# Longer q and k reads, reordered on the way out of PSUM, in a kernel of windowed attention and an ELU MLP

## The chip, the cores and the metric

One core of one Trainium2 chip runs the kernel. The metric is the device time of one execution in microseconds (us). Runs of one kernel agree within 2%. The calls ran on different chips, each with runs of the kernel before beside it; these stay within 401.3 to 409.0 us. The profile times are one profiled execution, about 2 us shorter than the run's own time.

Engine names in the profile: PE is TensorE (matmul), PEld its weight loads, DVE is VectorE, ACT is ScalarE, POOL is GpSimd, SP is SyncE, which issues DMAs. "PEclk" is the clock that TensorE was granted, 1.0 being full.

## The reference, cut to what matters

```python
batch, n_heads, seq, head_dim = 8, 8, 576, 64        # q, k, v: (8, 8, 576, 64) fp32
# down-sampled attention: q, k, v averaged over 4 tokens, 144 x 144 softmax, repeated 4 times
# local attention:        576 x 576 softmax, masked to |i - j| < 4
x = (out_up + out_local), to (8 * 576, 512)          # 4608 tokens
h = x @ w_in                                         # (512, 2048)
g = where(h > 0, h, exp(min(h, 0)) - 1)              # ELU
return g @ w_out                                     # (2048, 512)
```

Attention of a batch has to be done before the MLP can take the tokens of that batch. The kernel cuts the 4608 tokens into nine MLP tiles of 512. It works through the eight batches in pairs of heads (four pairs a batch).

## The kernel before

Q, k and v come in with one token of 64 fp32 values (256 B) as the contiguous run. Blocks of 96 tokens are transposed on TensorE by a matmul with the identity; the averages over four tokens are further columns of that same matmul. ScalarE and VectorE copy the results out of PSUM in the order in which they lie.

```python
ap=[[D, n], *blocks, [1, D]]                         # load: 256-byte runs, 96 tokens on 96 partitions
...
for c in range(NB):                                  # transposes; QI = identity | averages of 4
    nc.tensor.matmul(tq[:, c // 3, QW * (c % 3) : QW * (c % 3) + QW], q16[:, c, :, :], QI[:], ...)
...
nc.scalar.copy(out=qt[:], in_=tq[:, :, 0 : 3 * QW])
```

An MLP tile consists of 16 hidden blocks (`mm1`) and 16 output blocks (`mm2`), each of four matmuls of 512 columns. The hidden accumulator is one PSUM bank, and two of them are used in turn. Each is taken from the pool:

```python
def mm1(t, fc):
    ...
    tag = "misc" if t < 2 and fc % 2 else "hp"
    hp = ps.tile([128, TBLK], FP32, tag=tag, bufs=2, name="hp")
    for dc in range(DMC):
        nc.tensor.matmul(hp[:], WI[:, dc, 128 * fc : 128 * fc + 128], x[:, dc, :], ...)
    e = sb.tile([128, TBLK], FP16, tag="e", bufs=3, name="e")
    nc.scalar.activation(out=e[:], in_=hp[:], func=AF.Exp)
    nc.vector.tensor_scalar(out=e[:], in0=e[:], scalar1=1.0, scalar2=-1.0, op0=AB.min, op1=AB.add)
    nc.vector.scalar_tensor_tensor(out=gts[t][:, fc, :], in0=hp[:], scalar=0.0,
                                   op0=AB.max, in1=e[:], op1=AB.add)
```

Waits between engines are not written by hand: the tile framework records which instructions read and write each tile and puts in the semaphores. The program order on each engine is set by a list of events with times. Batches 1 to 7 are woven into the MLP of earlier tiles.

The softmax here doesn't subtract the row's maximum and nothing guards it: scores larger than these inputs give would overflow.

## Time and profile before

| | us |
|---|---|
| median of 2 runs | 404.04 (402.66 to 405.41) |
| profiled span | 401.8 |
| first hidden block with all its inputs | 48.6 |
| from when on TensorE is dense | about 141 |
| four matmuls of 512 columns, dense | 0.86 |

The stage view of the kernel before gives, for each stretch of the span, the busy time and number of instructions of each engine, then the granted clock, the DMA engines' busy share, and GB/s.

```profile
0.00:49.00 49.00, 22.97 (x252) 16.12 (x253) 13.87 (x25) 15.36 (x29) 24.74 (x35) 1.00 0.95 204
49.00:141.00 92.00, 75.81 (x741) 41.35 (x740) 61.88 (x109) 49.84 (x96) 43.96 (x56) 0.91 0.90 180
141.00:340.00 199.00, 196.45 (x1798) 102.14 (x1796) 153.06 (x275) 116.67 (x217) 70.03 (x96) 1.00 0.57 122
```

The first pair of numbers after the length is PE. TensorE is 99% busy from 141 to 340 us, so with the work of TensorE as it is, time can be won only before 141 us. DMA is nearly saturated up to 141 us, although it moves only 180 to 204 GB/s; most of its packets are under 512 B, as the next view shows.

The packet line of the page before and the rows of its group view that the change touches (engine, operation, output and inputs, count, then busy time and mean ns of one, then idle time before and what ended it):

```profile
DMA packets 138082, 53.81 MB, mean 134 GB/s; under 512 B 122580, under 2 KB 131388, under 8 KB 138044
L368 PE MATMUL hp<-xt,WI 128*128 128x512 f16 x576 | 150.9, 389 | 4.5 <-DVE gt L377 2.5 <-POOL xt L352 2.0
L182 ACT CAST qt<-tq 128x720 f16<-128x720 f32 x32 | 24.3, 760 | 30.7 <-PE tq L176 27.3 <-issue 2.3
L192 ACT CAST kt<-tk 128x612 f16<-128x612 f32 x32 | 21.8, 680 | 0.1
L263 DVE RECIPROCAL rc<-den 128x288 f16<-128x288 f32 x8 | 15.6, 1949 | 1.7 <-PE den L257 1.7
```

A copy out of PSUM costs about 0.7 us. The time line of TensorE shows the first hidden block getting its last input at 48.63 us and, late in the run with no attention left, hidden (`hp`) and output (`op`) blocks following each other every 0.86 us:

```profile
48.63 4.00 PE L368 MATMUL hp<-xt,WI 128*128 128x512 f16 x9 [0.69 <-POOL xt L352]
345.81 1.03 PE L368 MATMUL hp<-xt,WI 128*128 128x512 f16 x4
346.67 1.03 PE L388 MATMUL op<-WO,gt 128*128 128x512 f16 x4
347.54 1.03 PE L368 MATMUL hp<-xt,WI 128*128 128x512 f16 x4
```

### The profile page before, as it was taken

To read this page: it belongs to the slowest core of one execution; us is meant where nothing else is said; L and a number is where in the kernel's file an instruction comes from. 1 tells how busy PE (TensorE), PEld (TensorE's weight loads), DVE (VectorE), ACT (ScalarE), POOL (GpSimd) and SP (SyncE) were. 2 spreads that over 40 slices of the span, in tenths; PEclk is the share of its full clock that TensorE was granted. 3 is DMA by queue.
4 is the path that set the end of the run, shared out by engine and by line. 5 is a ranking of instruction groups with operands and counts; after the bars stand their busy time and mean duration, and the time that the engine had idled before them with its cause. 6 is when DMAs were issued, how large, how long until landed. Compare 5 with 4: busy or idle time off the path is not lost.

```text
span 401.8 us, 8092 instructions
## 1 busy us (share of the span) xinstructions
PE 353.0 (88%) x3052; PEld 185.6 (46%) x3052; DVE 254.4 (63%) x460; ACT 203.8 (51%) x377; POOL 138.7 (35%) x184
## 2 busy tenths in 40 slices
PE   1465688687986899999999999999899899999996
PEld 1352345343553455555545554555454444444442
DVE  0134599732586797697778769886886585555510
ACT  1462157535385376747564855667375334444321
POOL 3365755460850581075028304820450050000000
PEclk9999999968999799999999999999999999999999
DMA  6998999965966980796199639926820310100112
GB/s 121 189 253 258 190 215 234 265 126 134 198 139 130 189 176 16 172 231 125 28 195 217 118 78 194 226 64 121 172 79 33 102 53 28 49 29 28 52 54 78
DMA packets 138082, 53.81 MB, mean 134 GB/s; under 512 B 122580, under 2 KB 131388, under 8 KB 138044
## 3 DMA queue, kind: packets, MB, share of 16 engines
q1 hardware_dynamic: 129420, 47.62, 55.0%
q10 hardware_dynamic: 8624, 5.68, 6.6%
q8 instruction: 24, 0.39, 0.4%
q14 instruction: 14, 0.11, 0.1%
HBM read 43.33 MB, written 9.95 MB: 133 GB/s over the span
## 4 chain that ended last, share of the span: by engine, by line
PE 67%; DMA 12%; POOL 6%; issue 4%; DVE 4%; SPq 3%; ACTq 2%; ACT 1%; POOLq 0%; DVEq 0%
PE op L388 29%; PE hp L368 25%; PE sc L204 2%; PE tk L186 2%; PE tq L176 2%; DVE e L374 2%; PE tq L171 2%; PE lg L325 2%; POOL xt L352 2%; DMA w_170<-in_moe_w_in_dram 2%; DMA rcb<-rd 2%; SPq L149 2%; ACTq L276 2%; DMA w_161<-in_moe_w_in_dram 1%; DMA w_207<-in_moe_w_out_dram 1%
## 5 line engine op out<-in xcount | busy, mean ns | idle before, releaser
L368 PE MATMUL hp<-xt,WI 128*128 128x512 f16 x576 | 150.9, 389 | 4.5 <-DVE gt L377 2.5
L388 PE MATMUL op<-WO,gt 128*128 128x512 f16 x576 | 147.7, 385 | 4.7 <-POOL WO L119 3.8
L373 ACT ACTIVATE e<-hp 128x512 f16<-128x512 f32 x144 | 85.7, 601 | 109.5 <-PE hp L368 90.8
L377 DVE SCALAR_TENSOR_TENSOR gt<-hp,e 128x512 f16<-128x512 f32 x144 | 99.6, 692 | 5.4
L374 DVE TENSOR_SCALAR e<-e 128x512 f16<-128x512 f16 x144 | 63.8, 443 | 51.5 <-ACT e L373 50.5
L368 PEld LDWEIGHTS <-WI 128*128 128x128 f16 x576 | 54.5, 99 | 71.7 <-issue 13.4
L388 PEld LDWEIGHTS <-gt 128*128 128x128 f16 x576 | 54.6, 99 | 68.8 <-issue 7.6
L232 DVE TENSOR_TENSOR mex<-pex,MASK 102x1152 f16<-102x1152 f16 x32 | 29.6, 926 | 40.3 <-ACT pex L222 40.2
L352 POOL TENSOR_TENSOR xt<-ln,gn 128x512 f16<-128x512 f16 (+7 forms) x64 | 42.0, 688 | 34.7 <-DVE ln L343 34.7
L222 ACT ACTIVATE pex<-sc 102x576 f16<-102x576 f32 x64 | 41.4, 647 | 22.3 <-PE sc L214 22.3
L182 ACT CAST qt<-tq 128x720 f16<-128x720 f32 x32 | 24.3, 760 | 30.7 <-PE tq L176 27.3
L394 ACT COPY os<-op 128x512 f32<-128x512 f32 x36 | 21.2, 588 | 25.3 <-PE op L388 25.3
L204 PE MATMUL sc<-qt,kt 64*102 64x96 f16 x384 | 19.1, 226 | 11.5 <-DVE vd L184 6.0
L184 DVE CAST vd<-tq 72x256 f16<-72x256 f32 x32 | 13.2, 413 | 22.3 <-ACT qt L182 22.3
L204 PEld LDWEIGHTS <-kt 64*102 64x102 f16 x384 | 14.4, 135 | 25.8 <-ACT kt L192 12.6
L226 ACT ACTIVATE dex<-sc 72x288 f16<-72x288 f32 x64 | 25.8, 404 | 0.0
L343 DVE TENSOR_TENSOR ln<-lg,rcb 128x576 f16<-128x576 f32 x32 | 23.9, 748 | 0.0
L192 ACT CAST kt<-tk 128x612 f16<-128x612 f32 x32 | 21.8, 680 | 0.1
L176 PEld LDWEIGHTS <-VR 102*72 102x72 f16 x192 | 14.2, 123 | 5.7 <-issue 3.9
L263 DVE RECIPROCAL rc<-den 128x288 f16<-128x288 f32 x8 | 15.6, 1949 | 1.7 <-PE den L257 1.7
L340 DVE TENSOR_TENSOR gn<-lg,rcb 128x144 f16<-128x144 f32 x32 | 9.6, 301 | 5.7 <-POOL xt L352 3.0
L194 DVE CAST kd<-tk 128x144 f16<-128x144 f32 x32 | 9.6, 300 | 1.7 <-ACT kt L192 0.5
(361 smaller groups left out, 265.7 us busy)
## 6 DMA issues: line engine op xcount, KB each, us to landing
out_dram<-os SPq DMA_DIRECT2D x36, 256.0 KB
rcb<-rd ACTq DMA_DIRECT2D x14, 288.0 KB
rcb<-rd ACTq DMA_DIRECT2D x14, 72.0 KB
w_149<-in_moe_w_in_dram SPq DMA_DIRECT2D x1, 512.0 KB
w_152<-in_moe_w_in_dram SPq DMA_DIRECT2D x1, 512.0 KB
w_155<-in_moe_w_in_dram SPq DMA_DIRECT2D x1, 512.0 KB
w_158<-in_moe_w_in_dram SPq DMA_DIRECT2D x1, 512.0 KB
w_161<-in_moe_w_in_dram SPq DMA_DIRECT2D x1, 512.0 KB
```

What stands on the lines that cost most here:

```text
L182: nc.scalar.copy(out=qt[:], in_=tq[:, :, 0 : 3 * QW])
L204: nc.tensor.matmul(sc[e][0:KW, c // 3, QB * (c % 3) : QB * (c % 3) + QB], kt[r, c // 3, c % 3, :], qt[r, c // 3, QW * (c % 3) : QW * (c % ...
L222: nc.scalar.activation(out=pex[:, e, :].rearrange("p (g u) -> p g u", g=2), in_=sc[e][0:KW, :, 0:HB], func=AF.Exp, scale=SCALE,)
L226: nc.scalar.activation(out=dex[:, e], in_=sc[e][0:KG, :, HB : HB + SD], func=AF.Exp, scale=SCALE,)
L232: nc.vector.tensor_tensor(out=mex[:], in0=pex[:], in1=mk2, op=AB.mult)
L343: nc.vector.tensor_tensor(out=ln[:].rearrange("p (g u) -> p g u", g=2), in0=lg[:, :, 0:HB], in1=rcb[:, j, 0:S].rearrange("p (g u) -> p g u ...
L352: nc.gpsimd.tensor_tensor(out=xt(t)[:, j, t0 - TBLK * t : t1 - TBLK * t], in0=ln[:, a:z], in1=_rep4(gn[:, a // 4 : z // 4]), op=AB.add,)
L368: nc.tensor.matmul(hp[:], WI[:, dc, 128 * fc : 128 * fc + 128], x[:, dc, :], start=(dc == 0), stop=(dc == DMC - 1),)
L373: nc.scalar.activation(out=e[:], in_=hp[:], func=AF.Exp)
L374: nc.vector.tensor_scalar(out=e[:], in0=e[:], scalar1=1.0, scalar2=-1.0, op0=AB.min, op1=AB.add)
L377: nc.vector.scalar_tensor_tensor(out=gts[t][:, fc, :], in0=hp[:], scalar=0.0, op0=AB.max, in1=e[:], op1=AB.add)
L388: nc.tensor.matmul(op_[:], gts[t][:, fc, 128 * tt : 128 * tt + 128], WO[:, fc, :], start=(fc == 0), stop=(fc == FCN - 1),)
```

## The change

The intent is to shorten the front. Q and k are loaded with six consecutive tokens per partition (1.5 KB runs). The transposes then give token order "r, t" (token 6t + r), and the copy out of PSUM puts it right ("untangle"). Averages over four are no longer columns of the transposes but sums of the reordered tiles (on VectorE for batches 0 and 1, on GpSimd after that). Denominators are packed into 72 columns by 96 small matmuls, so that the reciprocal has 72 columns instead of 288. Batches 0 and 1 run by themselves, apart from the MLP, with hidden tile 0 between them. For that, PSUM is laid out by hand as four tiles of two banks, and the accumulators become halves of those.

```diff
-    def two(name):
-        return ps.tile([128, 2, 512], FP32, tag="two", bufs=2, name=name)
+    PA = ps.tile([128, 1024], FP32, tag="PA", bufs=1, name="PA")
+    PB = ps.tile([128, 1024], FP32, tag="PB", bufs=1, name="PB")
+    PM = ps.tile([128, 1024], FP32, tag="PM", bufs=1, name="PM")
+    PH = ps.tile([128, 1024], FP32, tag="PH", bufs=1, name="PH")
... (loads)
+                    ap=[[NR * D, NP], [S * D, 2], [1, NR * D]],
... (reordering copy)
+        copy(
+            out=qk[:, i, PAD : PAD + S].rearrange("p (t r) -> p r t", r=NR),
+            in_=tp[:, 0 : 128 * NR].rearrange("p (r t) -> p r t", r=NR)[:, :, 0:NP],
+        )
... (hidden blocks)
-        tag = "misc" if t < 2 and fc % 2 else "hp"
-        hp = ps.tile([128, TBLK], FP32, tag=tag, bufs=2, name="hp")
+        if t == 0:
+            hp = ((PH, PM)[fc % 2])[:, 512 * (fc // 2 % 2) : 512 * (fc // 2 % 2) + 512]
+        else:
+            hp = PH[:, 512 * (fc % 2) : 512 * (fc % 2) + 512]
... (order)
+    early(0, between0)
+    ...
+    for s in range(FCN):
+        mm1(0, s)
+    ...
+    early(1, lambda: None)
```

## The prediction

> **What bounds the kernel now.** The stage table (busy time in windows) shows two regimes. From 141 us to the end TensorE is 94 to 100% busy at full clock; the chain of waits there is almost only the two MLP matmul lines (four 512-column matmuls take 0.86 us, 215 ns each). A period of 16 hidden blocks, 16 output blocks and one batch of attention takes 37.7 us, 27.6 of it MLP, so about 10.1 us is one batch's attention. Nothing in the change shortens that. Nine tiles (248 us) and eight batches (81 us) need 329 us of the 402 us span; the other 73 us lie before 141 us: some 35 us before the first MLP block has all its inputs (48.6 us), because q, k, v arrive in 256-byte packets and TensorE did about 10 us of work, and some 25 us in 48 to 141 us (waits for casts, for DMA and for vd/kt copies, and granted clock 0.66 in 80 to 90 us, 0.83 in 120 to 140 us).
>
> **Front.** Before, a pair of heads arrived every 5 to 8 us (DMA share about 1.0 at 189 GB/s in 10 to 20 us, small halo transfers issued for 1.3 to 1.8 us each). 1.5 KB runs should go at about 300 GB/s (258 GB/s at share 0.85 for the 1 KB weight runs, 30 to 40 us); the Trainium skill, "DMA: Bandwidth & Descriptors", Specifications, asks for at least 512 B. Then q, k are in by about 12 us, v by 20. The loop over pairs is bound by VectorE: copy 0.76, sums of 4 about 1.3 (1152 elements at one per cycle: tensor_reduce has only the 1x mode by "VectorE: DVE Perf Modes", tier table; an estimate), mask 0.76, so about 3 us a pair. Sums, denominators (cold clock), spreading and outputs end near 37 us: the MLP starts about 10 us earlier.
>
> **Given back.** Hidden tile 0 runs alone, bound by VectorE (0.29 to 0.75 + 0.69 us a block): about 18 us for 13.8 of matmuls. Batch 1 is then done with no MLP beside it: four pairs at 3 us, denominators, spreading, outputs, about 26 us for 10 us of TensorE work; MLP tile 1 starts near 82 us. In front of batch 2 stand eight weight casts of 1.04 us on GpSimd, and its slots are one apart, so TensorE waits some 10 us more. Denominators become 96 small matmuls (16 of 144 columns took 0.36 us, 23 ns each): about +1 us a batch; narrower transposes save 0.5. The reciprocal falls from 1.95 to about 0.6 us, on an engine that does not bound. GpSimd sums (about 1.2 + 0.7 us) lengthen transposes-to-scores; that chain had about 0.8 us slack: 0 to 6 us in all.
>
> **Sum.** 82 + 298 dense + 4 tail + about 10 stall is 394 in the trace; retuned constants speak for less, stalls for more. Predicted median 393 us.
>
> **Right if** the profile shows the first hidden block fully fed at 34 to 41 us; packets under 512 B cut by more than half; TensorE under half busy for about 25 us between tile 0 and tile 1; then a stretch above 95%, at 37.5 to 39 us a period; reciprocal near 0.6 us.
>
> **Wrong if** batch 1 alone takes under 18 us or batch 2 does not stall (then 375 to 380), or if every scores block waits for the GpSimd sums (1 us each adds 20 us and it is slower than before), or if strided copies out of PSUM cost far more than 0.7 us.
>
> Chances: faster by over 2% 0.56, within 2% 0.33, slower 0.11. Range 375 to 409 us.

## The result, and the profile after

The changed kernel takes 603.9 us (601.09 and 606.71), against 404.04 us before. It is 1.496 times as slow, with a 95% interval of 1.475 to 1.517. Here and below, a ratio is the mean time of one kernel's fast runs over that of the other's fast runs in the same rounds, so it is not quite the ratio of the medians quoted.

The stage view of the kernel after, same columns:

```profile
0.00:40.00 40.00, 22.12 (x339) 16.53 (x340) 22.78 (x25) 21.26 (x31) 17.59 (x32) 1.00 0.90 253
88.00:160.00 72.00, 49.12 (x573) 27.39 (x572) 27.87 (x44) 42.37 (x53) 40.07 (x47) 0.67 0.46 121
160.00:460.00 300.00, 208.01 (x1933) 100.20 (x1932) 133.06 (x231) 156.12 (x203) 100.22 (x131) 0.90 0.28 75
460.00:599.00 139.00, 98.47 (x564) 41.55 (x562) 47.61 (x95) 35.59 (x61) 5.28 (x8) 0.99 0.10 34
```

The front did get shorter: the first hidden block has all its inputs at about 40 us, not 48.6. But the dense regime is gone. TensorE is 69% busy from 160 to 460 us and 71% from 460 us on, where hardly any attention is left. The page and the group view name two things:

```profile
DMA packets 73236, 53.34 MB, mean 89 GB/s; under 512 B 46842, under 2 KB 66410, under 8 KB 73194
L447 PE MATMUL PH<-xt,WI 128*128 128x512 f16 x544 | 160.8, 421 | 128.0 <-DVE gt L456 121.9 <-POOL xt L420 4.8
L214 ACT CAST qk<-PA 128x576 f16<-128x576 f32 x32 | 71.8, 2244 | 1.3 <-PE PA L208 1.3
L214 ACT CAST qk<-PB 128x576 f16<-128x576 f32 x24 | 50.2, 2090 | 13.5 <-PE PB L237 13.2
L230 POOL TENSOR_TENSOR s<-qk 128x576 f32<-128x576 f16 x24 | 27.5, 1144 | 172.2 <-ACT qk L214 172.2
```

First, the hidden blocks of TensorE waited 121.9 us for VectorE's `gt`, the last reader of the hidden accumulator; before it was 2.5 us. Second, the reordering copy takes 2.1 to 2.2 us instead of 0.7, and on ScalarE 24 + 32 of them are 122 us of work. The late time line of the kernel after, where no attention runs, shows the first of these alone (the top line is the first fully fed hidden block):

```profile
40.21 0.58 PE L447 MATMUL PH<-xt,WI 128*128 128x512 f16 x1 [0.69 <-POOL xt L420]
521.01 1.02 PE L447 MATMUL PH<-xt,WI 128*128 128x512 f16 x4 [0.88 <-DVE gt L456]
521.87 1.03 PE L467 MATMUL PM<-WO,gt 128*128 128x512 f16 x4
522.07 0.60 ACT L452 ACTIVATE e<-PH 128x512 f16<-128x512 f32 x1 [2.17 <-PE PH L447]
522.70 0.29 DVE L453 TENSOR_SCALAR e<-e 128x512 f16<-128x512 f16 x1 [1.74 <-ACT e L452]
523.02 0.69 DVE L456 SCALAR_TENSOR_TENSOR gt<-PH,e 128x512 f16<-128x512 f32 x1
523.77 1.02 PE L447 MATMUL PH<-xt,WI 128*128 128x512 f16 x4 [0.88 <-DVE gt L456]
```

Read it as a loop. A hidden block at 521.01, its exponential at 522.07, VectorE until 523.71, and only then the next hidden block at 523.77. The period is 2.76 us for a hidden and an output block, where it was 1.73. The accumulators alternate between two banks, so the next block need not wait for the reader of this one. The compiled program says that it was made to. I listed, for some hidden blocks, which VectorE instruction their semaphore wait stands for (this comes from building the kernels, not from the profile; offsets are in words of the tile, 512 being the second bank):

```
after:   matmul I-2425 writes PH at 512, waits for I-2393, which reads PH at   0
         matmul I-2463 writes PH at   0, waits for I-2432, which reads PH at 512
before:  matmul I-3723 writes hp_3722,   waits for I-3678, which reads hp_3670 (two blocks back)
         matmul I-3786 writes hp_3785,   waits for I-3691, which reads hp_3683 (two blocks back)
```

In the changed program a block waits for the reader of the other half, the block just before it. 128 hidden blocks of the changed program had a wait for such a reader, each for the other half of its own tile; in the kernel before 95 had one, each for an earlier tile. Two halves of one tile are no double buffer here.

### The profile page after: what moved, and what is told of

Read it like the earlier page. It is cut to its first block, busy times and chain, and to the rows that moved or that the text cites. A ratio compares the mean times of both kernels' runs of the same rounds, so it can differ in the third digit from the quotient of the medians.

```text
span 599.3 us, 8991 instructions
## 1 busy us (share of the span) xinstructions
PE 408.6 (68%) x3600; PEld 202.0 (34%) x3600; DVE 266.6 (44%) x440; ACT 279.8 (47%) x383; POOL 177.1 (30%) x234
## 4 chain that ended last, share of the span: by engine, by line
PE 33%; DVE 20%; ACT 20%; issue 8%; POOL 4%; DMA 1%; ACTq 0%; DVEq 0%; POOLq 0%
PE PH L447 17%; ACT qk L214 10%; PE PM L467 10%; DVE gt L456 9%; DVE e L453 7%; ACT e L452 7%; DVE ln L411 2%; PE PB L265 1%; POOL WO L145 1%; POOL xt L420 1%; ACT os L473 1%; DVE gn L408 1%; PE PB L237 1%; DMA v<-in_v_dram 1%; PE PB L277 1%
## 5 line engine op out<-in xcount | busy, mean ns | idle before, releaser
L447 PE MATMUL PH<-xt,WI 128*128 128x512 f16 x544 | 160.8, 421 | 128.0 <-DVE gt L456 121.9
L452 ACT ACTIVATE e<-PH 128x512 f16<-128x512 f32 x136 | 86.0, 633 | 224.7 <-PE PH L447 224.7
L467 PE MATMUL PM<-WO,gt 128*128 128x512 f16 x576 | 160.8, 409 | 7.8 <-DVE rc L337 4.4
L447 PEld LDWEIGHTS <-WI 128*128 128x128 f16 x576 | 58.3, 104 | 225.4 <-issue 175.9
L456 DVE SCALAR_TENSOR_TENSOR gt<-PH,e 128x512 f16<-128x512 f32 x136 | 94.1, 692 | 5.1
L230 POOL TENSOR_TENSOR s<-qk 128x576 f32<-128x576 f16 x24 | 27.5, 1144 | 172.2 <-ACT qk L214 172.2
L214 ACT CAST qk<-PA 128x576 f16<-128x576 f32 x32 | 71.8, 2244 | 1.3 <-PE PA L208 1.3
L214 ACT CAST qk<-PB 128x576 f16<-128x576 f32 x24 | 50.2, 2090 | 13.5 <-PE PB L237 13.2
L190 POOL CAST q<-q 96x768 f16<-96x768 f32 x32 | 27.1, 847 | 23.8 <-issue 19.7
L190 POOL CAST k<-k 96x768 f16<-96x768 f32 x32 | 27.5, 860 | 2.3 <-DMA k<-in_k_dram 2.2
L197 POOL CAST v<-v 112x768 f16<-112x768 f32 x32 | 26.6, 835 | 3.6 <-DMA v<-in_v_dram 3.6
```

The lines of the kernel that those rows point to most:

```text
L190: nc.gpsimd.tensor_copy(out=t[:], in_=st32.pop((n, b, j)).rearrange("p e (r d) -> p r e d", d=D))
L197: nc.gpsimd.tensor_copy(out=t[:], in_=st32.pop(("v", b, j)).rearrange("p (e c) d -> p c e d", e=2))
L214: copy(out=qk[:, i, PAD : PAD + S].rearrange("p (t r) -> p r t", r=NR), in_=tp[:, 0 : 128 * NR].rearrange("p (r t) -> p r t", r=NR)[:, :, ...
L230: nc.gpsimd.tensor_tensor(out=s2[:], in0=x[:, :, :, 0], in1=x[:, :, :, 1], op=AB.add)
L447: nc.tensor.matmul(hp, WI[:, dc, 128 * fc : 128 * fc + 128], x[:, dc, :], start=(dc == 0), stop=(dc == DMC - 1),)
L452: nc.scalar.activation(out=e[:], in_=hp, func=AF.Exp)
```

## The experiments

Theory A: the loss is mostly this wait on the other half of the tile. Theory B: the slow reordering copies alone, by delaying the exponentials on ScalarE. Theory C: the low granted clock (0.889 on average) is a cause by itself. The first four kernels ran on one chip, beside 405.34 us for the kernel before.

### Hidden and output accumulators as tiles of their own

The two-bank tiles PM and PH are given back after batch 1, and single-bank tiles take their place.

```diff
+    pe.close()
+    late["ps"] = ctx.enter_context(tc.tile_pool(name="pl", bufs=1, space=bass.MemoryType.PSUM))
...
-            hp = PH[:, 512 * (fc % 2) : 512 * (fc % 2) + 512]
+            hp = late["ps"].tile([128, 512], FP32, tag="hp", bufs=2, name="hp")[:]
```

(The output accumulator, formerly a half of PM, likewise.)

> From MLP tile 1 on, the hidden and output blocks get accumulators of their own (one PSUM tile per bank, two in turn), instead of the two halves of one two-bank tile. Theory A (the wait of a hidden block on the VectorE reader of the OTHER half, 122 us of waits in the profile, is the larger part of the loss): 604 falls to 470 to 510 us; in the stretch without attention (the last tile pair) a hidden plus an output block take 1.73 us again, not 2.76. What is left is the slow reordering copies (2.1 to 2.3 us on ScalarE). Theory B (the slow copies alone, by delaying the exponentials): under 30 us gained. Theory C (the lower granted clock, 0.889 mean, is the cause and not a result): nothing gained, 590 to 610.

Measured: 494.51 us, ratio 1.223 to before, and 109 us less than the changed kernel. The hidden blocks' wait for `gt` falls from 121.9 to 1.1 us. In the compiled program the waits now stand for readers two blocks back. This run gives the output blocks tiles of their own too; a later run changes the hidden ones alone. What is left hangs on the copies, as the waits list shows (after the group line of the hidden blocks: who waited for whom, us in total, times, longest):

```profile
L448 PE MATMUL hp<-xt,WI 128*128 128x512 f16 x512 | 146.6, 411 | 4.6 <-POOL xt L421 3.5 <-DVE gt L457 1.1
POOL s L231 <- ACT qk L215: 129.2, 24, 7.1
PE PB L278 <- POOL qkd L233: 30.5, 20, 1.5
PE PB L266 <- ACT qk L215: 15.6, 20, 2.2
```

TensorE (the last two lines) now waits for the copies and for the sums behind them. Theories B and C, as sole causes, are refuted. The mean granted clock was 0.899 (before this edit 0.889) while 109 us went away.

### The reordering copy, written densely

```diff
-            out=qk[:, i, PAD : PAD + S].rearrange("p (t r) -> p r t", r=NR),
-            in_=tp[:, 0 : 128 * NR].rearrange("p (r t) -> p r t", r=NR)[:, :, 0:NP],
+            out=qk[:, i, PAD : PAD + S].rearrange("p (t r) -> p t r", r=NR),
+            in_=tp[:, 0 : 128 * NR].rearrange("p (r t) -> p t r", r=NR)[:, 0:NP, :],
```

> The reordering copy walks the same elements in the other order: it writes q, k densely and reads PSUM at a stride of 128 words (same values). If the stride of 12 bytes of the 2-byte writes makes the copy slow: one copy falls from 2.24 us to about 0.65 to 0.8 us. If reordering itself or PSUM reading is slow: it stays near 2 us. Time: theory A says the block wait stays, 530 to 570 us; theory B says 400 to 430 us.

Measured: 510.03 us, ratio 1.262, and 94 us less than the changed kernel. The group view of this run:

```profile
L447 PE MATMUL PH<-xt,WI 128*128 128x512 f16 x544 | 146.6, 391 | 88.5 <-DVE gt L456 82.8 <-POOL xt L420 4.8
L214 ACT CAST qk<-PA 128x576 f16<-128x576 f32 x32 | 20.6, 645 | 1.1 <-PE PA L208 1.1
L214 DVE CAST qk<-PB 128x576 f16<-128x576 f32 x8 | 6.0, 753 | 8.1 <-PE PB L208 8.0
```

The same elements, walked so that the writes are dense and the reads of PSUM jump by 512 bytes, cost 0.645 us instead of 2.244 on ScalarE and 0.753 instead of 2.073 on VectorE. So the stride of the writes was slow, not the reordering and not the reading of PSUM. The time came out 20 us better than I had expected under theory A, and far from what theory B said. The block wait was also partly caused by exponentials that stood behind a copy on ScalarE: it fell from 121.9 to 82.8 us. The time line of the changed kernel shows one such case: a hidden block at 244.78 us, a copy of 2.30 us on ScalarE from 245.36, the exponential only at 247.28, and a wait of 3.21 us before the next hidden block instead of 0.88.

### Both

> Both edits. Theory A plus slow copies explain all of the loss: 385 to 410 us, as the prediction had it, with four 512-column matmuls at 0.86 us back to back from about 100 us on. If something else was mis-sized (the GpSimd sums in the chain from transposes to scores, batch 1 alone): 420 to 460 us.

Measured: 415.76 us (414.97 to 417.35), ratio 1.030, interval 1.021 to 1.038. Of the 200 us lost, both edits together bring back 188 us. Singly they bring 109 and 94; the sum, 203, is 15 us more. That fits the case just seen, where an exponential behind a slow copy also lengthens the block wait, so that either edit removes part of it. The result lies just above the first expected range and below the second: about 3% over the kernel before is still to be explained. Its stages:

```profile
0.00:35.00 35.00, 22.14 (x339) 16.25 (x340) 17.69 (x25) 15.84 (x31) 17.93 (x32) 1.00 1.02 285
58.00:88.00 30.00, 20.93 (x342) 15.38 (x341) 20.24 (x29) 13.06 (x29) 11.79 (x16) 0.59 0.37 119
88.00:160.00 72.00, 58.01 (x553) 29.82 (x552) 37.68 (x61) 33.54 (x66) 46.74 (x55) 0.82 0.58 157
160.00:340.00 180.00, 174.31 (x1990) 92.90 (x1988) 136.29 (x232) 105.85 (x198) 95.30 (x123) 1.00 0.44 118
```

From 160 us on TensorE is 97% busy again. The front is done at 35 us, and 58 to 88 us is batch 1 by itself, at a granted clock of 0.59, so that TensorE's 20.9 busy us there stand for less work: six transposes that took 0.42 us at 58.19 us took 0.66 us at 64.74.

### The kernel before, with its hidden accumulators as two halves of one tile

```diff
-        tag = "misc" if t < 2 and fc % 2 else "hp"
-        hp = ps.tile([128, TBLK], FP32, tag=tag, bufs=2, name="hp")
+        if t < 2 and fc % 2:
+            hp = ps.tile([128, TBLK], FP32, tag="misc", bufs=2, name="hp")
+        else:
+            nhp[0] += 1
+            hp = PH[:, 512 * (nhp[0] % 2) : 512 * (nhp[0] % 2) + 512]
```

> The kernel before with one edit: its hidden accumulators become the two halves of one two-bank tile (those of the first two tiles only for the even blocks). Theory A: slower by 60 to 120 us (465 to 525 us), with the last tile pair at 2.76 us per hidden plus output block. Theory B and C: within 2% of 404 us.

Measured: 498.97 us, ratio 1.234, 94 us more than 405.34. So 94 us are lost by these lines alone, with nothing else of the change. The late time line has the same loop of 2.76 us as the changed kernel:

```profile
431.03 1.02 PE L373 MATMUL PH<-xt,WI 128*128 128x512 f16 x4 [0.88 <-DVE gt L382]
431.89 1.03 PE L393 MATMUL op<-WO,gt 128*128 128x512 f16 x4
433.79 1.02 PE L373 MATMUL PH<-xt,WI 128*128 128x512 f16 x4 [0.88 <-DVE gt L382]
```

The mean granted clock of this run was 0.986, so theory C has no part in it. Both directions, taking the halves away and putting them in, agree on about 100 us.

### What strides cost a copy

24 pairs of copies of 192 fp32 values per partition, from PSUM to SBUF, appended to the kernel with both edits. It ran once, in an unknown state.

> e3, with 24 pairs of copies of 192 fp32 values per partition out of PSUM appended after the last block: fp16 outputs at strides of 1, 2, 3, 4, 6, 8, 12, 16, 32 elements, fp32 outputs at 1, 2, 6, on ScalarE and on VectorE. If the 12-byte stride of the writes is what cost 2.24 us: about 1.0 us a copy at stride 6 against 0.37 dense on ScalarE (2.8 ns more an element), and a clear step at some smaller stride. If a narrow write is slow at every stride over 1, stride 2 is already slow; if fp32 at stride 6 is slow too, it is the stride in bytes and not the 2-byte element.

All copies of one form from the group view (`h` is fp16, `f` is fp32, the number is the stride in elements; ScalarE only; VectorE's means for fp16 are within 3 ns of these from stride 2 on):

```profile
L625 ACT CAST h1a<-PA 128x192 f16<-128x192 f32 x2 | 0.6, 322 | 0.0
L625 ACT CAST h2a<-PA 128x192 f16<-128x192 f32 x2 | 0.7, 373 | 0.9 <-DVE h1d L625 0.9
L625 ACT CAST h4a<-PA 128x192 f16<-128x192 f32 x2 | 1.2, 584 | 1.1 <-DVE h3d L625 1.1
L625 ACT CAST h6a<-PA 128x192 f16<-128x192 f32 x2 | 1.6, 796 | 1.4 <-DVE h4d L625 1.3
L625 ACT CAST h8a<-PA 128x192 f16<-128x192 f32 x2 | 2.0, 1007 | 1.8 <-DVE h6d L625 1.7
L625 ACT CAST h32a<-PA 128x192 f16<-128x192 f32 x2 | 2.0, 991 | 2.1 <-DVE h16d L625 2.1
L632 ACT COPY f2a<-PA 128x192 f32<-128x192 f32 x2 | 0.7, 328 | 0.9 <-DVE f1d L632 0.9
L632 ACT COPY f6a<-PA 128x192 f32<-128x192 f32 x2 | 1.0, 494 | 0.9 <-DVE f2d L632 0.9
```

Stride 6 adds (796 - 322) / 192 = 2.5 ns an element; for the 576 elements of the real copy that is 1.4 us, near the 1.6 us seen. There is no step at one stride: the cost grows steadily from stride 2 to 8 (16 bytes) and is flat beyond that. The size of an element matters too. At the same 8 bytes fp16 costs 584 ns and fp32 328, and at 24 bytes fp16 costs 999 (stride 12) and fp32 494. The Trainium skill, "SBUF — State Buffer", Specifications, gives SBUF 16-byte lines, with at least two hits a line for full bandwidth. The end of the growth at 16 bytes and the free fp32 stride of 2 agree with it; fp16 at stride 4 (two hits a line, and yet 1.8 times the dense copy) does not.

### Weight casts in the idle time of batch 1

The eight GpSimd casts of the output weights stood in front of batch 2, where the trace of the kernel with both edits shows TensorE waiting 2.1 + 3.5 us for q and v casts (its waits from 84 to 160 us):

```profile
PE PB L238 <- POOL v L198: 3.5, 1, 3.5
PE PB L209 <- POOL q L191: 2.1, 1, 2.1
```

This run moves them into batch 1's stretch.

```diff
-    early(1, lambda: None)
+    def between1():
+        for i in range(12, 16):
+            wload(i)
+        for i in range(8, 16):
+            wcast(i)
+
+    early(1, between1)
```

> e3, with the eight casts of the output weights moved from the start of MLP tile 1 into batch 1's stretch, where GpSimd is idle for 15.7 us. The prediction charged about 10 us to batch 2's wait behind these casts; the trace of e3 shows 2.1 + 3.5 us of TensorE waits there and a cold clock after them. Expected 405 to 410 us (e3 was 415.8); if the waits only move on to the next cast or load, 413 to 417 us.

Measured: 415.59 us, ratio 1.027, interval 1.020 to 1.035: nothing gained. The two waits are gone, but batch 1 ends 8 us later (tile 1 begins at 93.1 us, with both edits at 85.1). Its time line says why:

```profile
64.08 3.14 POOL L198 CAST v<-v 112x768 f16<-112x768 f32 x4
65.16 9.56 DVE L306 TENSOR_TENSOR mex<-pex,MASK 112x1152 f16<-112x1152 f16 x1
67.16 8.45 POOL L146 CAST WO<-w 128x1024 f16<-128x1024 f32 x8
74.64 0.74 DVE L215 CAST qk<-PB 128x576 f16<-128x576 f32 x1
```

The masking product, normally 0.75 us (median 0.76 of the 32 in this run), took 9.56 us: it went on until GpSimd's row of casts was nearly over. The Trainium skill, "SBUF — State Buffer", Who interferes with whom, says that a VectorE instruction with two SBUF inputs contends with GpSimd's reads for a shared pair of ports, an exclusive lock held for the whole instruction. The trace agrees with the contention. But no hand-over at the end of one GpSimd instruction is to be seen: VectorE's 9.56 us span about ten back-to-back GpSimd casts of 0.8 to 1.1 us. Who held the lock when is inferred; the profile doesn't record it.

### The same casts on ScalarE

```diff
+        for i in range(8, 12):
+            wcast(i, nc.scalar)
+    early(1, between1)
+    for i in range(12, 16):
+        wcast(i, nc.scalar)
```

> e3, with the eight casts of the output weights in batch 1's stretch as in e5, but on ScalarE. In e5 the masking product (two SBUF operands on VectorE) took 9.56 us beside GpSimd's back-to-back casts instead of 0.75, and batch 1's stretch became 8 us longer, which ate the gain. If that contention is the cause: 403 to 410 us (e3 415.8, e5 415.6) and no masking product over 2.5 us; if something else held e5 back: 413 to 418.

Measured: 410.58 us (408.76 to 414.21), ratio 1.017, interval 1.008 to 1.026. That is about 5 us under the two kernels before it, though on another chip, with a kernel before of 404.57, and the intervals of the three ratios overlap. Four of the eight casts now stand after batch 1, and not in its stretch. The traces say more than the times. The longest masking product is 2.11 us, as it was with both edits:

```profile
L306 DVE TENSOR_TENSOR mex<-pex,MASK x32: 747/759/2109, 13.1 to 313.8; 112x1152 f16<-112x1152 f16 x32
```

(The three times are the shortest, the median and the longest, in ns.) Tile 1 begins at 85.8 us instead of 93.1, and the two waits for q and v casts stay gone. So the contention was what had lengthened batch 1's stretch in the previous run.

### Batch 1 woven into the MLP again

The kernel with both edits keeps batch 0 of the change, but takes the old order for batches 1 to 7. With it go two more changes, so that the place of batch 1 is not the only difference: the loads are issued in another order, and hidden tile 0 gets accumulators of its own (before, it still used halves of PH and PM).

```diff
-    early(1, lambda: None)
-    def start_of(t):
-        return 16 * (t - 1)
-    for b in range(2, B):
+    def start_of(t):
+        return 0 if t == 0 else 16 * (t + 1)
+    for b in range(1, B):
+        base = start_of(b) - 26.5
+        slots, d0, o0 = SLOTS, 16.1, (22.5, 24.1)
... (loads issued in the order of the casts, up to 11 buffers ahead)
```

> e3 (both edits), with batch 1 no longer alone between MLP tiles 0 and 1 but woven into the MLP as in the kernel before (the old schedule for batches 1 to 7; batch 0 stays the changed kernel's). Theory: what is left of the loss in e3 is batch 1 alone (58 to 88 us of its trace) plus the waits and the cold clock up to 160 us; the loads themselves made the front 13 us shorter (fully fed at 35 us, before at 48.6). Then this is 385 to 398 us, faster than before. Rival: the front's gain is lost anyway, because the GpSimd sums lengthen the chain from transposes to scores and the woven stretch becomes slower by as much: 403 to 418 us.

Measured: 393.08 us (389.44 to 396.19), ratio 0.968, interval 0.959 to 0.976: faster than before. One of the four runs (396.19) was slow and is not in the ratio. The first fully fed hidden block is at 35.5 us instead of 48.6, and of those 13.1 us the profiled spans keep 11.6 (401.8 - 390.2):

```profile
35.48 4.81 PE L446 MATMUL hp<-xt,WI 128*128 128x512 f16 x16 [0.69 <-POOL xt L421]
```

So 13 us is what the new front was worth: the longer runs together with the new order of batch 0. The longer runs by themselves, in the kernel before, were not tried. What this run undid cost more than that, 23 us.

### And its weight casts on ScalarE

In that trace, VectorE's short step of the ELU (min and add on `e`, in SBUF) took up to 2.7 us beside GpSimd's casts, instead of 0.29, between 40 and 48 us.

```diff
-        wcast(i)
+        wcast(i, nc.scalar if i % 2 else None)     # input weights 4 to 7
...
-        wcast(i)
+        wcast(i, nc.scalar)                        # output weights 8 to 15
```

> e4, with the eight casts of the output weights and two of the last four of the input weights on ScalarE instead of GpSimd. In e4's trace VectorE's two-operand and fast copies beside back-to-back GpSimd casts took 1.5 to 2.7 us instead of 0.29 (40 to 48 us). If GpSimd's casts hold VectorE up there, the stretch from 35 to 80 us gets shorter and the time falls from 393 to 382 to 390 us; if ScalarE's own queue now delays the exponentials by as much, 391 to 398.

Measured: 387.73 us, ratio 0.956, interval 0.945 to 0.966; one of the four runs (391.79) was slow and is not in the ratio. This is the best, 4.4% faster than the kernel before. The step from the previous kernel is within the noise, since the two intervals overlap and the chips differ; the trace shows the intended effect. Between 40 and 80 us VectorE's busy time fell from 28.9 us (37 instructions) to 19.9 us (38).

## Why the prediction was right or wrong

The prediction, 393 us with a range up to 409, was wrong by 211 us. The step that failed is its sum, "82 + 298 dense + 4 tail + about 10 stall is 394". The 298 took it as given that TensorE would run as densely as before, and the 82 rested on "copy 0.76".

- **"298 dense".** Wrong, and the largest part. The prediction says nothing of the accumulators. From the first fully fed block of tile 1 (98.4 us) the changed kernel needed 501 us. I had read the halves of PH in the diff as the same double buffer as before. The compiled program waits for the other half. Taking that away brought 109 us, putting it into the kernel before cost 94 us.
- **"Copy 0.76".** Mis-sized threefold: 2.07 us on VectorE and 2.24 on ScalarE, from a write stride of 12 bytes. The text named it as a way to be wrong ("if strided copies out of PSUM cost far more than 0.7 us") but did not count it in the sum. Alone it was worth 94 us, with the wait above included in part.
- **"The MLP starts about 10 us earlier."** Right. Fully fed at about 40 us with the slow copies, at 35.1 with dense ones; packets under 512 B fell from 122580 to 46842. The skill's advice on runs of at least 512 B ("DMA: Bandwidth & Descriptors", Specifications) fits: 285 GB/s in the front with both edits, 204 before. No run here tries a size near 512 B.
- **Hidden tile 0 alone, "about 18 us".** Low: 23 us in the changed kernel (40.2 to 63.3) and with both edits (35.1 to 58.3), two blocks every 2.76 us. The sum counted VectorE's work alone. These blocks use the halves of PH and PM in turn, and each has to wait for the reader of the other half of its tile, two blocks back; that is the first fault again, and the kernel with both edits still has it in this tile.
- **Batch 1 alone, "about 26 us", and tile 1 "near 82 us".** A little low: 58 to 88 us with both edits, at about 3 us a pair as predicted (60.3 to 73.4 us for four). But TensorE was not "under half busy": it was busy for 62% of 63 to 98 us in the changed kernel and 70% with both edits, at granted clocks of 0.55 and 0.59, which the prediction did not count there. In the changed kernel, with slow copies, tile 1 was fully fed at 98.4.
- **"TensorE waits some 10 us more" behind the weight casts.** The waits were 5.6 us with both edits. Moving the casts on GpSimd gained nothing, on ScalarE about 5 us, which is not clear of the noise.
- **96 small matmuls, "about +1 us a batch".** Wrong in sign. They take 0.90 us (132.22 to 133.12 us with both edits), against 1.09 us before (192.73 to 193.82).
- **Reciprocal near 0.6 us, sums of 4 about 1.3, GpSimd sums 1.2 + 0.7 us.** Right: 0.61, 1.35 and 1.14 + 0.67. The last hardly held TensorE up with dense copies (one such wait of 1.7 us from 84 to 160 us, none from 160 to 330).
- **A period of "37.5 to 39 us".** A tile has 64 hidden matmuls. In the changed kernel 300 of them took the 300 us from 160 to 460 us, 64 us a tile. With both edits 265 took the 160 us from 160 to 320 us, about 38.6 us a tile.

With the two faults out of the rest of the run, the sum of 394 was 20 us short of the trace of the kernel with both edits (413.5). Tile 1 was fully fed at 87.9 us instead of 82, which is 6 of them (5 in tile 0, 4 in batch 1, less 2 or so for the earlier front). The other 14 came after it: from 88 to 160 us TensorE was busy for 58 of 72 us, at a granted clock of 0.82 and with the wait behind the casts, and after that a tile took 38.6 us where the sum had about 37 (298 for eight). The run with batch 1 woven in again won 23 us with the same 1.5 KB loads and with GpSimd doing the sums of all batches but the first, so neither of these cost it; but that run also freed tile 0's accumulators and changed the order of the loads. How the 20 us divide between these, the clock and the waits was not separated. That this run took 393 us, the number predicted for another kernel, is chance. Nor is it known what the changed kernel would do with its waits drawn per half, since a wait could not be edited by itself.

## What to carry to other kernels

Before counting halves of a tile as two buffers, find out from the compiled waits, or from one late stretch of the profile, what the framework orders. Where each matmul block waits for the last reader of the block just before it, at a fixed period longer than its own work (2.76 us against 1.73 here), there is only one buffer. When a copy has to reorder, let the strided side be the read of PSUM and keep 2-byte writes dense. And work moved into the "idle" time of GpSimd was not free while VectorE had two-operand products from SBUF to do (9.56 us for one of 0.75); ScalarE was the better place here.

## What the Trainium skill lacked or had wrong

- "SBUF — State Buffer", Specifications and the note on lines of 16 bytes: it says that two hits a line are enough for full bandwidth, and that one can stride for free up to 8 bf16 elements. For 2-byte writes from PSUM the runs show 322 ns dense, 373, 584, 796 and 1007 at strides of 2, 4, 6 and 8, flat after that. For fp32 it holds at stride 2 (328 against 319), the only one up to 4 that was tried.
- "SBUF — State Buffer", Who interferes with whom: the lock is said to be held for the whole instruction, the other engine being blocked until then. In one run a 0.75 us masking product of VectorE took 9.56 us beside about ten GpSimd casts in a row.
- "TensorE: Matmul & The Clock Gate", Part 1, says that successive matmuls never start less than about 25 ns apart. 96 matmuls of 72 columns, in four column groups of 32, took 0.90 us, 9.4 ns each; the page "TensorEngine Tiling (Array Packing)" gives the speed-up of column groups only as a factor of up to 4.
- "PSUM — Partial Sum Buffer" warns of non-contiguous access for matmuls and says nothing of the other readers. A ScalarE copy that reads PSUM at 512-byte steps took 0.645 us for 576 values, no more than the dense copy of 612 values before (0.680).
- No page says that two accumulators in one tile may be ordered as one. Here that cost 94 to 109 us.
